# A delta-rule recurrence whose inverse times v is added up in PSUM, diagonal blocks placed by ScalarE, and a first channel product in 15 for 18 block products in three chunks

## The chip, the cores and the metric

The kernel runs on one core of one Trainium2 chip. The metric is device time of the whole program in microseconds, as the median of repeated runs; lower is better. Lines L... are lines of the kernel before, unless "of after" is said.

## The reference

The program is an attention block of delta-rule type and a mixer behind it, all in float32. B = 4 batches, H = 8 heads, S = 768 tokens, D = 48; the model width is H * D = 384, the hidden width 1536.

```python
k_n = k / (norm(k) + 1e-6)
state = 0                                   # per batch and head, D x D
for t in range(S):
    y[t] = q[t] @ state
    state += beta[t] * outer(k_n[t], v[t] - k_n[t] @ state)
x = y, heads side by side                   # (B, S, 384)
u = x + (x.T @ U @ V).T                     # U: S x 32, V: 32 x S
out = u + relu(u @ w_ch1) @ w_ch2           # 384 -> 1536 -> 384
```

## The kernel before

**The recurrence.** The tokens of a batch are cut into 12 chunks of 64 (c = 0 to 11); six chunks make a unit, and the units are n = 0 to 7, two per batch. A unit is loaded (`load`), its keys and queries are turned (`turn`, `turn_blocks`) and multiplied into 64 x 64 blocks (`products`, L700 to L746), the blocks' triangular systems are inverted (`blocks`, L814 and L820 on VectorE; `joins`, L871 to L932 on TensorE), and the inverses are put together in `pg` (`diagonals`, L950; L938). `products` also picks the 32 x 32 diagonal blocks out of PSUM into `diag`: ScalarE takes the even ones through a mask (L721), VectorE adds the odd ones through another mask (two instructions, L724), and after it ScalarE copies the whole product (L731), which gives the PSUM banks back.

`prepare` (L1024 to L1062) multiplies, for three chunks at a time, the inverses with the keys (L1034, copied by ScalarE at L1053) and with the values (L1045, copied by ScalarE at L1058 over `vn`). `recur` (L1064 to L1125) then goes through the chunks: 8 small matmuls of state with keys (L1083), VectorE subtracts them from the prepared values into `z` (L1096), 8 matmuls of z with keys (L1111), VectorE adds them to the state (L1122). `outputs` (L994 and L1008) multiplies the state and z with the queries beside it; `put` copies that into X on ScalarE (L978).

**The mixer.** `front` adds the low-rank part to X and turns a piece of 256 tokens (i = 0 to 2 of batch b; here called a chunk b.i) into `ut` (L1437 to L1483). For the chunks of batches 0 to 2, `wide` does the two channel products. The first (`channels`, L1537) is 12 blocks of 128 hidden channels by 3 blocks of the width by 256 tokens: 36 matmuls of 128x128 with 256 columns, two hidden blocks to a step; ScalarE applies the relu from PSUM into `hs` (L1502). `add_up` (L1560) makes sums S1 and S2 of `hs`, and `narrow` (L1645) does the second product in seven block products for eight (42 matmuls of 192 columns); `gather` (L1573) adds them to X. Batch 3 is done last, in another way: its first product is already made in 15 block products for 18 (`quick`, L1351), with sums of weights (`weight_sums`, L1292) and sums of tokens (`token_sums`, L1323), where each block product is read out of PSUM as soon as it is made, by ScalarE (L1376, L1365) or by VectorE, which adds it to another block (L1382); its second product is L1769.

**What sets the order.** Each piece of work is a Python generator that yields one step at a time: an engine, a PSUM bank to take, banks to give back. Which generator goes on next is written out by hand in one long list (`ORDER`, L144 on): at each position stands the name of a generator, and its next instructions are recorded there. So every engine's instruction order is fixed by that list; semaphores are put in where one engine reads what another wrote, and where two engines touch the same bank of PSUM. PSUM has 8 banks: up to four pairs for the recurrence and the products (three once the mixer runs), and two single ones ("mix", banks 6 and 7) for the mixer.

**Forms on TensorE.** The mixer's matmuls use the whole 128 x 128 array. The recurrence's use quarters of 64 x 64, four at a time, and `joins` sixteenths of 32 x 32. A float32 matmul appears in the trace as two records, each with its weight load (PEld).

Of the kernel before, what the change touches and what calls it, by code (L numbers as in the profile page):

```python
# [17 lines left out]
BK = 32  # L18
SB = 16
DP = 64  # L20
GT = 256
# [6 lines left out]
def kernel(  # L28
# [116 lines left out]
    add_up b0 i0 f00: 594 612 668; add_up b0 i0 f03: 632 645 667; add_up b0 i1 f00: 793 820 841; add_up b0 i1  # L145
    f03: 846 859 861; add_up b0 i2 f00: 1028 1035 1036; add_up b0 i2 f03: 1037 1045 1046; add_up b1 i0 f00: 1165
    1167 1194; add_up b1 i0 f03: 1200 1202 1206; add_up b1 i1 f00: 1324 1351 1354; add_up b1 i1 f03: 1359 1362
    1366; add_up b1 i2 f00: 1511 1513 1548; add_up b1 i2 f03: 1541 1543 1556; add_up b2 i0 f00: 1679 1693 1740;
    add_up b2 i0 f03: 1704 1719 1738; add_up b2 i1 f00: 1868 1869 1872; add_up b2 i1 f03: 1889 1893 1900; add_up
    b2 i2 f00: 2004 2039 2048; add_up b2 i2 f03: 2049 2051 2054; blocks n0: 61 73 75 76 82 84 86 88 89 91 93 94  # L150
    96 97 103 110 114 122; blocks n1: 143 157 160 163 173 175 179 192 201 206 208 212 213 215 218 219 226 229;
    blocks n2: 479 498 510 513 514 518 520 524 526 528 529 532 536 538 539 541 542 544; blocks n3: 691 708 710
    711 714 716 718 720 721 722 733 740 744 748 752 755 756 760 768 769 771 785 788 792 794 797 798 799 800 801
    802 824 825 826; blocks n4: 937 941 942 944 948 951 964 965 966 967 975 977 979 1003 1004 1009 1017 1019
    1038 1067 1084 1085 1086 1088 1114 1115 1116 1117 1118 1119 1120 1121 1122 1138; blocks n5: 1143 1171 1173
    1174 1175 1204 1217 1221 1231 1232 1243 1244 1245 1257 1262 1266 1274 1277 1286 1287 1289 1292 1293 1294
    1295 1300 1304 1307 1309 1325 1332 1348 1349 1350; blocks n6: 1484 1490 1491 1492 1505 1506 1516 1527 1532
    1536 1540 1549 1554 1573 1579 1583 1584 1588 1592 1607 1608 1612 1617 1632 1636 1643 1645 1646 1647 1649
    1650 1664 1671 1673; blocks n7: 1676 1695 1696 1703 1711 1712 1720 1737 1741 1747 1749 1773 1778 1779 1784
    1786 1788 1792 1797 1807 1810 1811 1813 1817 1818 1819 1822 1825 1826 1827 1828 1841 1842 1848; channels b0  # L160
    i0 e0: 546 547; channels b0 i0 e1: 551 552; channels b0 i0 e2: 553 555; channels b0 i0 e3: 556 567; channels
    b0 i0 e4: 568 588; channels b0 i0 e5: 597 600; channels b0 i1 e0: 738 743; channels b0 i1 e1: 759 761;
    channels b0 i1 e2: 775 778; channels b0 i1 e3: 796 805; channels b0 i1 e4: 822 829; channels b0 i1 e5: 830
    832; channels b0 i2 e0: 924 927; channels b0 i2 e1: 932 934; channels b0 i2 e2: 936 939; channels b0 i2 e3:
    960 972; channels b0 i2 e4: 992 994; channels b0 i2 e5: 995 1008; channels b1 i0 e0: 1131 1132; channels b1
    i0 e1: 1133 1134; channels b1 i0 e2: 1136 1144; channels b1 i0 e3: 1158 1160; channels b1 i0 e4: 1161 1166;
    channels b1 i0 e5: 1184 1185; channels b1 i1 e0: 1278 1282; channels b1 i1 e1: 1284 1310; channels b1 i1 e2:
    1311 1313; channels b1 i1 e3: 1314 1315; channels b1 i1 e4: 1323 1333; channels b1 i1 e5: 1343 1344;
    channels b1 i2 e0: 1455 1458; channels b1 i2 e1: 1477 1479; channels b1 i2 e2: 1489 1493; channels b1 i2 e3:
    1494 1495; channels b1 i2 e4: 1503 1504; channels b1 i2 e5: 1520 1524; channels b2 i0 e0: 1641 1642;  # L170
    channels b2 i0 e1: 1653 1654; channels b2 i0 e2: 1655 1667; channels b2 i0 e3: 1681 1682; channels b2 i0 e4:
    1683 1684; channels b2 i0 e5: 1686 1687; channels b2 i1 e0: 1814 1816; channels b2 i1 e1: 1835 1836;
    channels b2 i1 e2: 1837 1840; channels b2 i1 e3: 1844 1845; channels b2 i1 e4: 1846 1847; channels b2 i1 e5:
    1871 1874; channels b2 i2 e0: 1947 1948; channels b2 i2 e1: 1955 1974; channels b2 i2 e2: 1981 1990;
    channels b2 i2 e3: 2002 2011; channels b2 i2 e4: 2022 2029; channels b2 i2 e5: 2037 2041; cut f0 f00 k0 to1:
    2153; cut f0 f00 k1 to0: 2182; cut f0 f00 k1 to1: 2123; cut f0 f00 k2 to0: 2171; cut f0 f00 k2 to1: 2186;
    cut f1 f03 k0 to1: 2206; cut f1 f03 k1 to0: 2244; cut f1 f03 k1 to1: 2251; cut f1 f03 k2 to0: 2241; cut f1
    f03 k2 to1: 2245; cut f2 f06 k0 to1: 2169; cut f2 f06 k1 to0: 2181; cut f2 f06 k1 to1: 2130; cut f2 f06 k2
    to0: 2168; cut f2 f06 k2 to1: 2170; cut f3 f09 k0 to1: 2220; cut f3 f09 k1 to0: 2243; cut f3 f09 k1 to1:
    2242; cut f3 f09 k2 to0: 2247; cut f3 f09 k2 to1: 2249; diagonals n0 h0: 188 190 191 195 210 222; diagonals  # L180
    n0 h1: 167 169 171 176 181 186; diagonals n1 h0: 312 315 319 336 343 353; diagonals n1 h1: 290 292 303 338
    349 358; diagonals n2 h0: 598 599 622 628 634 638; diagonals n2 h1: 647 651 672 697 703 724; diagonals n3
    h0: 863 890 891 892 893 899; diagonals n3 h1: 879 880 881 889 931 933; diagonals n4 h0: 1151 1159 1176 1193
    1205 1208; diagonals n4 h1: 1180 1224 1225 1228 1239 1254; diagonals n5 h0: 1391 1392 1393 1410 1411 1412;
    diagonals n5 h1: 1364 1396 1416 1420 1443 1471; diagonals n6 h0: 1714 1715 1724 1742 1757 1768; diagonals n6
    h1: 1709 1710 1716 1744 1746 1756; diagonals n7 h0: 1919 1921 1922 1928 1929 1930; diagonals n7 h1: 1857
    1859 1860 1884 1906 1907; front b0 i0: 495 502 503 515 516 519; front b0 i1: 523 561 591 602; front b0 i2:
    636 652 678 682; front b1 i0: 1058 1059 1068 1070 1076 1078; front b1 i1: 1108 1153 1196 1210; front b1 i2:
    1381 1403 1424 1426; front b2 i0: 1587 1591 1610 1614 1624 1635; front b2 i1: 1639 1644 1668 1690; front b2
    i2: 1751 1761 1764 1775; front b3 i0: 2038 2040 2042 2045 2046 2052; front b3 i1: 2053 2057 2060 2062; front  # L190
    b3 i2: 2063 2068 2071 2073; gather b0 i0 h0 c0 k0: 677; gather b0 i0 h0 c0 k1: 680; gather b0 i0 h0 c1 k6:
    737 871; gather b0 i0 h1 c0 k2: 693; gather b0 i0 h1 c0 k5: 734 926; gather b0 i0 h1 c1 k3: 706; gather b0
    i0 h1 c1 k4: 715; gather b0 i1 h0 c0 k0: 862; gather b0 i1 h0 c0 k1: 847; gather b0 i1 h0 c1 k6: 916 925;
    gather b0 i1 h1 c0 k2: 873; gather b0 i1 h1 c0 k5: 913 1170; gather b0 i1 h1 c1 k3: 876; gather b0 i1 h1 c1
    k4: 887; gather b0 i2 h0 c0 k0: 1031; gather b0 i2 h0 c0 k1: 1066; gather b0 i2 h0 c1 k6: 1110 1281; gather
    b0 i2 h1 c0 k2: 1075; gather b0 i2 h1 c0 k5: 1111 1296; gather b0 i2 h1 c1 k3: 1082; gather b0 i2 h1 c1 k4:
    1087; gather b1 i0 h0 c0 k0: 1203; gather b1 i0 h0 c0 k1: 1229; gather b1 i0 h0 c1 k6: 1270 1623; gather b1
    i0 h1 c0 k2: 1233; gather b1 i0 h1 c0 k5: 1272 1560; gather b1 i0 h1 c1 k3: 1237; gather b1 i0 h1 c1 k4:
    1258; gather b1 i1 h0 c0 k0: 1365; gather b1 i1 h0 c0 k1: 1375; gather b1 i1 h0 c1 k6: 1448 1689; gather b1
    i1 h1 c0 k2: 1405; gather b1 i1 h1 c0 k5: 1449 1707; gather b1 i1 h1 c1 k3: 1409; gather b1 i1 h1 c1 k4:  # L200
    1423; gather b1 i2 h0 c0 k0: 1578; gather b1 i2 h0 c0 k1: 1572; gather b1 i2 h0 c1 k6: 1634 1798; gather b1
    i2 h1 c0 k2: 1593; gather b1 i2 h1 c0 k5: 1631 1688; gather b1 i2 h1 c1 k3: 1606; gather b1 i2 h1 c1 k4:
    1615; gather b2 i0 h0 c0 k0: 1731; gather b2 i0 h0 c0 k1: 1739; gather b2 i0 h0 c1 k6: 1808 1870; gather b2
    i0 h1 c0 k2: 1762; gather b2 i0 h1 c0 k5: 1812 2134; gather b2 i0 h1 c1 k3: 1776; gather b2 i0 h1 c1 k4:
    1781; gather b2 i1 h0 c0 k0: 1901; gather b2 i1 h0 c0 k1: 1892; gather b2 i1 h0 c1 k6: 1940 2072; gather b2
    i1 h1 c0 k2: 1913; gather b2 i1 h1 c0 k5: 1942 2216; gather b2 i1 h1 c1 k3: 1916; gather b2 i1 h1 c1 k4:
    1918; gather b2 i2 h0 c0 k0: 2050; gather b2 i2 h0 c0 k1: 2058; gather b2 i2 h0 c1 k6: 2088 2218; gather b2
    i2 h1 c0 k2: 2067; gather b2 i2 h1 c0 k5: 2086 2197; gather b2 i2 h1 c1 k3: 2070; gather b2 i2 h1 c1 k4:
# [1689 lines left out]
```

## Time and profile before

| | |
|---|---|
| median of 3 runs | 589.99 us (589.21 to 590.24) |
| the profiled execution | 589.53 us |
| its span in the trace | 587.7 us |
| instructions | 23435 |
| granted TensorE clock, mean of the span | 0.944 |

The span is the time from the first to the last instruction of the trace; 1.8 us of the execution lie outside it. A busy TensorE in the page is not TensorE at its peak: the ends of matmuls are modelled, and in the records a matmul's time reaches into the next one's. For its pace one takes the distance from start to start, or the length of a run of equal instructions in the chain of waits, divided by their count. In the page's table of 40 slices one slice is 14.7 us.

### The profile page before, as it was taken

How to read it: one execution, taken by the hardware profiler on the slowest of the kernel's cores; microseconds unless marked ns; L12 is line 12 of the kernel's file. 1: busy time of each engine (PE TensorE's matmuls, PEld its weight loads, DVE VectorE, ACT ScalarE, POOL GpSimd, SP SyncE). 2: the span in 40 equal slices, each digit the busy share in tenths (PEclk: the TensorE clock that was granted, in tenths of full speed). 3: DMA queues.
4: the chain of work that ended last, by engine and by line, in shares of the span. 5: the costliest groups of instructions: out<-in, count | busy, mean ns of one | idle time of the engine just before them, and what ended most of it. 6: DMA issues, size and time to landing. Idle time of an engine off the chain costs nothing.

```text
span 587.7 us, 23435 instructions
## 1 busy us (share of the span) xinstructions
PE 553.4 (94%) x10404; PEld 476.9 (81%) x10404; DVE 441.9 (75%) x1051; ACT 217.9 (37%) x444; POOL 133.4 (23%) x229
## 2 busy tenths in 40 slices
PE   3788887899999999999999999999999999999996
PEld 3688876588989987989989888899889868755996
DVE  3888757899998587897885479999874225789941
ACT  2846575526323432054134331144333421345000
POOL 8122045044016406042041405044030000000000
PEclk9665567999999999999999999999999999999999
DMA  9960638532015216022220404231020000100001
GB/s 142 196 164 24 217 91 203 123 86 45 14 25 105 53 35 113 11 53 55 53 47 13 81 16 90 56 89 34 3 66 30 3 3 1 41 0 2 0 15 67
DMA packets 89396, 36.21 MB, mean 62 GB/s; under 512 B 75408, under 2 KB 87056, under 8 KB 89296
## 3 DMA queue, kind: packets, MB, share of 16 engines
q1 hardware_dynamic: 80752, 24.69, 19.9%
q0 software_dynamic: 6944, 9.74, 7.6%
q8 instruction: 81, 1.33, 1.0%
q10 hardware_dynamic: 1600, 0.30, 0.3%
q14 instruction: 19, 0.16, 0.1%
HBM read 29.98 MB, written 4.72 MB: 59 GB/s over the span
## 4 chain that ended last, share of the span: by engine, by line
PE 81%; DVE 12%; issue 2%; ACT 2%; DMA 1%; SPq 0%; DVEq 0%; ACTq 0%
PE P L1537 23%; PE P L1645 21%; PE P L1769 7%; PE P L1351 6%; PE P L711 4%; PE P L1083 2%; DVE xt L820 2%; DVE prod L814 2%; PE P L1111 2%; PE P L885 2%; PE P L871 2%; PE P L1045 2%; PE P L1008 2%; PE P L1034 2%; PE P L994 2%
## 5 line engine op out<-in xcount | busy, mean ns | idle before, releaser
L1537 PE MATMUL P<-ut,w_sb 128*128 128x256 f32 x648 | 151.3, 386 | 0.0
L1537 PEld LDWEIGHTS P<-ut,w_sb 128*128 128x128 f32 x648 | 119.6, 190 | 17.9 <-issue 1.2
L1645 PE MATMUL P<-w_sb,hs 128*128 128x192 f32 x540 | 94.1, 329 | 0.0
L1645 PEld LDWEIGHTS P<-w_sb,hs 128*128 128x128 f32 x540 | 87.5, 190 | 2.6 <-issue 1.2
L820 DVE TENSOR_TENSOR xt<-xt,prod 128x112 f32<-128x112 f32 (+21 forms) x200 | 64.6, 323 | 6.9
L814 DVE TENSOR_TENSOR prod<-gs,xt 128x112 f32<-128x112 f32 (+21 forms) x200 | 63.4, 317 | 3.6
L1502 ACT ACTIVATE hs<-P 128x512 f32<-128x512 f32 x54 | 32.1, 596 | 80.4 <-PE P L1537 69.3
L978 ACT COPY X<-P 64x192 f32<-64x192 f32 x96 | 30.0, 313 | 72.4 <-PE P L1008 71.2
L566 POOL DMA_DIRECT2D slot<-in_v_dram x32 | 21.1, 666 | 75.9 <-DVE prod L814 49.7
L1645 PE MATMUL P<-w_sb,S 128*128 128x192 f32 x216 | 38.0, 330 | 0.0
L1096 DVE TENSOR_TENSOR z<-slot,P 128x192 f32<-128x192 f32 x44 | 15.5, 353 | 29.8 <-PE P L1083 29.2
L1645 PEld LDWEIGHTS P<-w_sb,S 128*128 128x128 f32 x216 | 34.8, 190 | 2.1 <-issue 1.2
L1573 DVE TENSOR_TENSOR X<-X,P 128x192 f32<-128x192 f32 x63 | 21.5, 346 | 18.6 <-PE P L1645 18.1
L552 POOL DMA_DIRECT2D slot<-in_k_dram x40 | 25.0, 630 | 44.3 <-DVE z L1096 22.4
L950 ACT COPY slot<-zz 32x384 f32<-32x384 f32 x64 | 32.3, 508 | 3.0 <-DVE zz L889 2.1
L711 PEld LDWEIGHTS P<-slot 48*64 48x64 f32 x1536 | 29.3, 151 | 4.7 <-issue 1.9
L711 PE MATMUL P<-slot 48*64 48x64 f32 x1536 | 32.4, 238 | 0.7 <-DVE slot L742 0.7
L566 POOL DMA_DIRECT2D slot<-in_k_dram x44 | 29.7, 677 | 7.9 <-PE P L1111 7.6
L957 POOL MEMSET slot<- 32x384 f32 x32 | 13.0, 411 | 72.3 <-PE P L914 70.2
L552 POOL DMA_DIRECT2D slot<-in_q_dram x40 | 24.5, 619 | 18.6 <-DVE slot L758 10.5
L799 POOL MEMSET xt<- 128x1056 f32 x8 | 7.9, 984 | 86.9 <-DVE zz L827 86.8
L1122 DVE TENSOR_TENSOR s<-s,P 128x192 f32<-128x192 f32 x40 | 13.9, 348 | 13.0 <-PE P L1111 10.1
(180 smaller groups left out, 1001.5 us busy)
## 6 DMA issues: line engine op xcount, KB each, us to landing
w_sb<-in_moe_w_ch_dram SPq DMA_DIRECT2D x10, 384.0 KB, 5.5
out_dram<-X SPq DMA_DIRECT2D x19, 192.0 KB, 2.5
slot<-in_k_dram SPq DMA_DIRECT2D x48, 72.0 KB, 3.4
slot<-in_k_dram POOLq DMA_DIRECT2D x44, 72.0 KB, 3.3
slot<-in_v_dram SPq DMA_DIRECT2D x32, 72.0 KB, 3.3
slot<-in_v_dram POOLq DMA_DIRECT2D x32, 72.0 KB, 2.8
X<-in_moe_w_ch_dram SPq DMA_DIRECT2D x6, 384.0 KB, 4.5
wide<-in_moe_w_ch_dram SPq DMA_DIRECT2D x6, 384.0 KB, 5.1
```

What stands on the lines that cost most here:

```text
L552: queue.dma_start(out=blocked(n)[quarter(y % 4), j, g, :, 0:w], in_=src[b, 4 * g + 2 * j + par, hf * UC * L : (hf + 1) * UC * L, BK * low ...
L566: queue.dma_start(out=t[half(1 - g if name == "z" else g), :, to, 0:D], in_=src[b, 4 * g + s, hf * UC * L : (hf + 1) * UC * L, :].rearrang ...
L711: nc.tensor.matmul(p_g[half(g ^ (par * i)), par, c], kq[rows, c, j, 0, half(g)], kq[rows, c, j, i, half(g)], start=True, stop=True,)
L814: nc.vector.tensor_tensor(out=prod, in0=gb[:, :, j : j + 1, j + 1 :].to_broadcast([128, split, m, w]), in1=xb[:, :, 0:m, j : j + 1].to_bro ...
L820: nc.vector.tensor_tensor(out=xb[:, :, 0:m, j + 1 :], in0=xb[:, :, 0:m, j + 1 :], in1=prod, op=ALU.subtract,)
L950: nc.scalar.copy(pg[quarter(i), :, at, :, a : a + BK], cut(zc, h)[quarter(i)].rearrange("p r (c j) t -> p r c j t", j=2),)
L978: nc.scalar.copy(x[half(c % 2), c // 2, 4 * D * g : 4 * D * (g + 1)].rearrange("p (j r d) -> p r j d", r=2, d=D), states(p_y)[half(g)],)
L1351: nc.tensor.matmul(to, forms[h][w][:, g] if isinstance(w, str) else w1_of(*w, h)[:, g], TOKENS[t] if isinstance(t, str) else u_of(*t), sta ...
L1502: nc.scalar.activation(hs[:, fs[0] : fs[1] + 1 : fs[1] - fs[0]], p_f, ACTF.Relu)
L1537: nc.tensor.matmul(p_f[:, x], w(x, t), ut[:, t], start=(t == 0), stop=(t == KT - 1))
L1645: nc.tensor.matmul(to, of[0], of[1], start=of[2], stop=of[3], skip_group_check=True)
L1769: nc.tensor.matmul(p[:, m], a[:, h, 128 * m : 128 * m + 128], v[:, h, j], start=fresh and m == h == j == 0, stop=(j == h == 1), skip_group ...
```

## The change

For batches 1 to 3 (`JOINT = 1`), and units n from 2, three things are done otherwise; in three chunks of the mixer a fourth.

1. `prepare` no longer multiplies the inverses with the values, and the copy of the keys' product gets a factor of -1. A new part `values(c)` makes that product chunk by chunk, straight into the PSUM bank in which `recur` then adds its own 8 matmuls. VectorE's subtraction into z is replaced by a ScalarE copy out of PSUM. The matmuls of z with keys go into other columns of the bank that the next chunk's `values` has taken, so no bank of their own is taken.
2. For units n from 3, the diagonal blocks are copied by four ScalarE instructions of 32 partitions, in place of one masked ScalarE instruction and two on VectorE.
3. Chunk 2.2's first channel product is made in 15 block products for 18 for both halves of the hidden blocks, chunks 1.2 and 2.1 for one half (`FAST`). Each block product is two matmuls of 128 columns (`fifteen`), into one bank per half, where two chains of sums take 256 columns each; each is read at once by ScalarE or VectorE (`seen`), relus are separate ScalarE instructions on `hs` (`limit`), and the sums of tokens are made by 8 VectorE instructions per chunk in S1 and S2 (`tokens`). The sums of weights are those that batch 3 uses.
4. `ORDER` is written anew from position 497 on: 2479 positions for 2326.

```diff
@@ products (units n > 2)
-                yield op("act", act(384) + 0.1, rush=True)
-                nc.scalar.mul(to, p_g[:, :, :, 0:BK], even[:, 0:1])
-                for r in range(2):
+                if n > NU * JOINT:
+                    for y in range(4):
+                        a = BK * (y % 2)
+                        yield op("act", act(384))
+                        nc.scalar.copy(to[quarter(y)], p_g[quarter(y), :, :, a : a + BK])
...
@@ prepare
+            if n >= NU * JOINT:
+                yield op("act", act(768), give=[("pair", x)])
+                nc.scalar.mul(
+                    kq[:, cs[0] : cs[2] + 1, :, 0].rearrange("p c j (g t) -> p (c j) g t", g=2),
+                    p_k.rearrange("p g c j t -> p (c j) g t"), -1.0,
+                )
+                emitted(("ready", n, h), 0.1)
+                return
@@ recur
+        def values(c):
...
+            x = yield op("pe", 0.23, "Q", take="pair", words=32, flow=0.16)
+            sums[c] = x
+            for j, par, g in heads:
+                nc.tensor.matmul(
+                    states(pair(x)[:, :, 0 : 2 * D])[half(g ^ par), par, j],
+                    zt[half(g), par, cu, j],
+                    vn[half(g), cu, 2 * par + j],
+                    start=(j == 0),
+                    stop=(c == 0),
+                    skip_group_check=True,
+                )
+            emitted(("values", b, c))
...
+            if b >= JOINT:
+                yield need(("values", b, c))
+                xb = sums[c]
+                p_b = pair(xb)[:, :, 0 : 2 * D]
+                if c > 0:
...
+                        nc.tensor.matmul(
+                            states(p_b)[half(g ^ par), par, j],
+                            kq[half(par, D), cu, j, 0, half(g)],
+                            states(s_old)[half(par, D), g, j],
+                            start=False,
...
+                yield op("act", act(192), give=[("pair", xb)], rush=True)
+                z = zs[c] = small.tile([128, 4, D], FP32, name="z", bufs=3)
+                nc.scalar.copy(z.rearrange("p (r j) d -> p r (j d)", r=2), p_b)
...
+                if b >= JOINT:
+                    yield need(("values", b, c + 1))
+                    p_s = pair(sums[c + 1])[:, :, 2 * D : 4 * D]
@@ the mixer's first product
+    FAST = {(1, 2): (0,), (2, 1): (0,), (2, 2): (0, 1)}
+    CHAINS = (
+        ((4, 0, 1, 1), (10, 2, 0, -1), (12, 1, 0, 1), (13, 1, 0, 1), (2, 1, 1, -1), (7, 0, 1, -1), (14, 2, 1, 1),
+         (5, 2, 0, -1), (11, 0, 0, 1)),
+        ((1, 1, 1, 1), (6, 0, 1, 1), (9, 1, 1, 1), (0, 1, 0, -1), (3, 2, 0, 1), (8, 2, 1, -1)),
+    )
+    OPENING, PUT = (4, 10, 13), (12, 14, 4, 1, 10)
...
+        def fifteen(h, k):
+            bank = h if len(quickly) == 2 else 0
...
+            p = mixed(bank)[:, GT * k : GT * k + GT].rearrange("p (g n) -> p g n", g=2)
+            for z, (e, r, m, sign) in enumerate(CHAINS[k]):
...
+                    *[("seen", b, i, h, CHAINS[k][z - 1][0])] * (z > 0),
...
+                yield op("pe", 0.432, "F", take=("mix", bank) if z == k == 0 else None, words=8)
+                for g in range(2):
+                    nc.tensor.matmul(
+                        p[:, g],
...
+                        start=e in OPENING and g == 0, stop=g == 1, skip_group_check=True,
+                    )
...
+        def seen(h, e, p, r, m, sign, give):
+            to = hs[:, HF * h + r : HF * h + r + 4 : 3, 128 * m : 128 * m + 128]
+            if e == 11:
...
+                nc.scalar.activation(to, p, ACTF.Relu)
...
+            elif e in PUT:
+                yield op("act", act(256), rush=True)
+                nc.scalar.mul(to, p, float(sign))
...
+                begin(limit(h, r, m, to), 3)
+            else:
+                yield need(("put", b, i, h, r, m))
+                yield op("dve", dve(256), rush=True)
+                nc.vector.tensor_tensor(out=to, in0=to, in1=p, op=ALU.add if sign > 0 else ALU.subtract)
...
+        def limit(h, k, j, at):
...
+            yield op("act", act(256))
+            nc.scalar.activation(at, at, ACTF.Relu)
```

Counted in the two built programs, in instructions: on TensorE 72 matmuls of 128x128 with 256 columns go and 120 with 128 columns come; the 288 matmuls of the inverses with the values are as many as before, in groups of 8 for 24. On VectorE 33 subtractions into z and 20 masked additions go, 36 reads of block products and 24 sums of tokens (8 per chunk) come. On ScalarE 12 copies of prepared values, 10 masked diagonal copies and 12 relus go; 36 copies into z, 40 diagonal copies, 20 copies, 20 relus and 4 relus out of PSUM of block products come. DMAs are the same in number and size. TensorE changes between forms (whole array, quarters, sixteenths) 162 times for 169; its order is the same up to the first matmul of the mixer's first product.

More of the change, by code (lines that the diff above doesn't have):

```diff
@@ L155 @@
[L155 to L159, printed above, removed]
@@ L1062, in prepare @@
             emitted(("ready", n, h), 0.1)
+        sums = {}
+        def values(c):
+            n, cu = NU * b + c // UC, c % UC
+            _, _, zt, _, _, vn, _, _ = units[n]
+            yield need(
+                *[x for h in [cu // 3] for x in (("upper", n, h), ("diagonal", n, h))],
+                ("grams", n), ("scaled", n), *[("placed", b, c - 2)] * (c > 1),
+            )
[11 more added lines that the diff above has]
+            emitted(("values", b, c))
         zs = {}
+        if b >= JOINT:
+            for c in range(NC):
+                begin(values(c), 60)
         for u in range(NU):
@@ new lines, in limit, with rows, add_up @@
+        def limit(h, k, j, at):
+            yield need(*[("seen", b, i, h, x) for c in CHAINS for x, r, m, _ in c if (r, m) == (k, j)])
+            yield op("act", act(256))
+            nc.scalar.activation(at, at, ACTF.Relu)
+            for g in range(2):
+                emitted(("h", b, i, HF * h + 3 * g + k, j), 0.06)
+        def rows(k, m, f0=0, n=HF):
+            return [("h", b, i, HF * k + f, m) for f in range(f0, f0 + n)]
+        def add_up(f0):
+            yield need(
+                *rows(0, 1, f0, 3), *rows(1, 1, f0, 3), *rows(0, 0, f0, 3),
+                *[("made", b, i, h, e) for h in quickly for e in (8, 11)],
+            )
@@ L1638, in narrow @@
             else:
-                for x, y in enumerate(ys):
-                    if x:
+                for z, (x, y) in enumerate(turns):
+                    if z:
                         yield need(*SECOND[y][2])
@@ L1652, in narrow @@
                 emitted(("narrow", b, i))
-        for e in range(len(PAIRS)):
+        begin(made())
+        for e in range(len(plain)):
             begin(channels(e), 95)
+        for h in quickly:
+            for k in range(2):
+                begin(fifteen(h, k), 95)
+        for f0 in range(0, HF, 3):
+            begin(add_up(f0), 4)
         begin(last_sum(), 4)
@@ L1857 @@
             for i in range(NG):
+                if (b, i) in FAST:
+                    begin(tokens(b, i), 97)
                 begin(wide(b, i), 95)
```

562 lines of the change are left out of this document (333 added, 229 removed).

## The prediction

> **What bounds the kernel now.** I read the page first, then the chain of waits in order of time, the groups by form, the waits of TensorE, and one step of the timeline.
>
> ```profile
> PE 553.4 (94%) x10404; PEld 476.9 (81%) x10404; DVE 441.9 (75%) x1051; ACT 217.9 (37%) x444; POOL 133.4 (23%) x229
> ...
> PE   3788887899999999999999999999999999999996
> ...
> DVE  3888757899998587897885479999874225789941
> ...
> PEclk9665567999999999999999999999999999999999
> ...
> PE 81%; DVE 12%; issue 2%; ACT 2%; DMA 1%; SPq 0%; DVEq 0%; ACTq 0%
> ```
>
> From the ninth slice on TensorE is never under 9 tenths, at full clock. That alone does not say that it works and does not wait. The pace of equal runs does; here is the chain of waits for the whole span:
>
> ```profile
> 360.20 1.41 PE P L711 x96
> ...
> 464.45 1.49 PE P L1537 x6
> ...
> 467.27 1.49 PE P L1537 x6
> ...
> 487.85 0.66 PE P L1480 x6
> ...
> 521.34 22.33 PE P L1351 x68
> 543.66 37.06 PE P L1769 x228
> 581.16 2.23 PE P L1769 x12
> ```
>
> A record of 192 columns takes 37.06 / 228 = 0.1625 us, one of 384 columns 22.33 / 68 = 0.328 with a gap or two, one of 128 columns (L1480, transposes) 0.66 / 6 = 0.11. The line through these is 0.833 ns a column and 2.5 ns, so 256 columns take 0.216 and 128 take 0.109. Six records of L1537 should then last 1.30, and each of the short runs lasts 1.49: a change of form costs 0.19 to 0.20.
>
> With these paces I add up TensorE from the first matmul of L1537, at 114.92, to the end of the last of L1769, at 583.39:
>
> ```profile
> 114.92 9.33 PE L1537 MATMUL P<-ut,w_sb 128*128 128x256 f32 x42
> ```
>
> 648 records of L1537 at 0.216 are 140.0; 756 of L1645 and 240 of L1769 at 0.1625 are 161.9; 120 of L1351 at 0.3225 are 38.7; 2176 matmuls in quarters, two records each at the 14.7 ns of L711 (1.41 / 96) and some longer, are 69; sixteenths, transposes and the 32-column form, at their own runs' paces, another 26; 145 changes of form at 0.2 are 29. The sum is 464.6, and the stretch is 468.5. So only some 4 us of it are waits. What the change does to the time is what it does to TensorE's own stream, and what waits it puts into it; work of the other engines counts only through such waits.
>
> **Part 1, the first product in 15 for 18.** 72 matmuls of 256 columns go: 144 records at 0.216 are 31.1 us. 120 of 128 columns come: 240 records. Whether they run at 0.109 the trace of before does not show, since each needs its own weight load:
>
> ```profile
> L1537 PE MATMUL P<-ut,w_sb 128*128 128x256 f32 x648 | 151.3, 386 | 0.0
> L1537 PEld LDWEIGHTS P<-ut,w_sb 128*128 128x128 f32 x648 | 119.6, 190 | 17.9 <-issue 1.2
> ...
> L711 PEld LDWEIGHTS P<-slot 48*64 48x64 f32 x1536 | 29.3, 151 | 4.7 <-issue 1.9 <-ACT slot L698 1.3 <-DVE slot L742 0.9
> ```
>
> A load record is 190 ns long, but its length is no pace: the loads of L711 are 151 ns long, and a quarter takes one each 59 ns (four quarters at 14.7), with 64 columns of weights and 64 of data, where the stream alone would ask for 53. So load and stream overlap when they are equally long, at a cost of about 6 ns. I take 0.112 for the record of 128 columns: 240 are 26.9. Bounds: 26.2 (0.109) and 45.6 (0.190). Part 1 is worth -4.2 us (-4.9 to +14.5). The Trainium skill, page "TensorE: Matmul & The Clock Gate", section "LDWEIGHTS (loading the stationary operand)", puts a load at columns over 1.2 per ns, 107 ns for 128; as an estimate from it load and stream are level, and the sum would be -4.9.
>
> **Part 2, changes of form.** In the built program they are 162 for 169, all seven after 114.92: -1.4 us (0 to -1.4).
>
> **Part 3, the recurrence.** The matmuls are the same in number, so TensorE's work is unchanged. What can change is the wait between them:
>
> ```profile
> PE P L1008 <- DVE z L1096: 1.2, 4, 0.3
> PE P L994 <- DVE s L1122: 1.1, 2, 0.6
> ...
> PE P L1083 <- DVE s L1122: 1.0, 3, 0.5
> ...
> PE P L1111 <- DVE z L1096: 0.8, 2, 0.5
> ```
>
> One step, in the timeline:
>
> ```profile
> 465.88 0.45 PE L1083 MATMUL P<-s,slot 48*64 48x48 f32 x16
> ...
> 466.46 0.35 DVE L1096 TENSOR_TENSOR z<-slot,P 128x192 f32<-128x192 f32 x1 [1.53 <-PE P L1083]
> ...
> 466.87 0.40 PE L1111 MATMUL P<-z,slot 64*48 64x48 f32 x16
> ```
>
> Here z starts 0.13 after the matmuls end (466.33), lasts 0.35, and 0.06 later TensorE goes on. Two groups of outputs (0.23 each) stand between and cover 0.46 of these 0.54. After, a ScalarE copy out of PSUM takes the subtraction's place, and `values` (0.23) is a third group that mostly stands there.
>
> ```profile
> L950 ACT COPY slot<-zz 32x384 f32<-32x384 f32 x64 | 32.3, 508 | 3.0 <-DVE zz L889 2.1
> ...
> L978 ACT COPY X<-P 64x192 f32<-64x192 f32 x96 | 30.0, 313 | 72.4 <-PE P L1008 71.2
> ...
> L1096 DVE TENSOR_TENSOR z<-slot,P 128x192 f32<-128x192 f32 x44 | 15.5, 353 | 29.8 <-PE P L1083 29.2
> ...
> L724 DVE SCALAR_TENSOR_TENSOR slot<-P,even,slot 128x192 f32<-128x192 f32 x32 | 12.0, 406 | 6.7 <-ACT slot L721 6.7
> ...
> L1058 ACT COPY slot<-P 128x576 f32<-128x576 f32 x16 | 10.2, 638 | 0.9 <-PE P L1045 0.7
> ...
> L721 ACT ACTIVATE slot<-P,even 128x384 f32<-128x384 f32 x16 | 9.2, 582 | 23.0 <-PE P L711 22.8
> ```
>
> The copy takes 0.313 for 0.353, so the way is 0.50 against 0.69 of cover: the wait for z goes. Of the 4.1 us in those four rows about half belong to batches 1 to 3: -2.0 us (0 to -3). ScalarE gets 36 x 0.313 = 11.3 more and 12 x 0.638 = 7.7 less; VectorE loses 33 x 0.353 = 11.6. What is late next is a ScalarE copy that stands behind something long; that is a rival below.
>
> **Part 4, the diagonal blocks.** 20 VectorE instructions at 0.406 go (8.1 us); ScalarE gets 40 at about 0.5 (row L950, from SBUF) and loses 10 at 0.582: +14. No TensorE instruction is added. In `products` the four copies (2.0) stand where 0.58 + 2 x 0.41 = 1.4 stood, so a pair of banks is held 0.6 longer, ten times. I cost it at nothing, since other work stands on TensorE meanwhile; without that cover 10 x 0.6 = 6 us (0 to +6).
>
> **Part 5, the waits that the 15 products bring.** This is the part against the change. Each product is read before the next of its chain overwrites it, and both chains of a half lie in one bank. In the built program a product waits for the reads of that bank that stand before it in the written order, the other chain's too. The Trainium skill, page "PSUM — Partial Sum Buffer", section "PSUM bank collisions raise a hardware error", says why: two engines must not touch one bank and quadrant at once, whatever the address. No run here shows a collision. What a read costs when nothing covers it:
>
> ```profile
> L1382 DVE TENSOR_TENSOR slot<-slot,P 128x384 f32<-128x384 f32 x36 | 19.0, 550 | 5.4 <-PE P L1351 2.9 <-ACT slot L1376 2.1
> ...
> L1376 ACT ACTIVATE slot<-P 128x384 f32<-128x384 f32 x20 | 9.1, 489 | 16.7 <-PE P L1351 16.7
> ```
>
> Between 0.35 for 192 columns and 0.55 for 384, a VectorE read of 256 is 0.42 (ScalarE 0.37). With 0.13 before and 0.06 after, an uncovered read stops TensorE for 0.6 us. In the order of after most of the 60 products have 1.3 us of L1537's successor or a group of the recurrence between; five wait for the read of the product right before them (one at the start and one later in chunk 1.2, one in 2.1, two in 2.2), and two have a single product (0.45) between. That is 5 x 0.6 + 2 x 0.15 = 3.3 us. Reads also queue: VectorE is full where chunk 1.2 is made, and in 2.2 the reads stand in front of the state's addition, for which the recurrence waits.
>
> ```profile
> 360.00:380.00 20.00, 20.00 (x326) 16.77 (x318) 19.20 (x48) 2.74 (x6) 1.45 (x3) 1.00 0.33 69
> 380.00:400.00 20.00, 19.88 (x227) 17.25 (x227) 18.56 (x51) 10.32 (x20) 8.41 (x14) 1.00 0.35 79
> 460.00:480.00 20.00, 19.70 (x539) 15.72 (x540) 7.20 (x20) 7.60 (x20) 0.00 (x0) 1.00 0.01 3
> ```
>
> (The columns after the length are TensorE, its loads, VectorE, ScalarE.) Chunk 1.2's 9 reads and 8 sums of tokens (128 to 384 columns, on the line through rows L1096 and L1382) are 3.8 + 3.1 = 6.9 us of VectorE where 1 or 2 in 20 are free, against 4.2 of subtractions gone per batch. Chunk 2.2 falls into the third row, where VectorE has 12 us of 20 free. I put 1.7 on this queueing: part 5 is +5.0 us. Bounds: +1 (most of the five covered by work that the profile can't show) and +12 (each of some twenty tight products stops TensorE once).
>
> **The sum.** -4.2 - 1.4 - 2.0 + 0 + 5.0 = -2.6. The profiled execution took 589.53, so 586.9; it lies 0.46 under the median of 589.99, so on the median's footing 587.4. The stretch before 114.92, where TensorE shows 3 to 8 tenths, is left as it is; TensorE's order is the same there.
>
> **The rivals.**
>
> (a) *The reads of the 15 products bound three chunks.* In one bank TensorE and readers take turns, so a product costs 0.45 + 0.6 unless other work stands between. The gain of parts 1 to 3 is 7.6 us, so it decides from 13 uncovered products on (13 x 0.6 = 7.8). At 20 of 60 it is +12 - 7.6 = +4.4: 594 us, slower. For it: the full VectorE of 360 to 400, and the waits across chains in the built order. Against it: the order puts L1537's successor or the recurrence between most pairs. Chance 0.19.
>
> (b) *Loads pace the short matmuls* at 0.190 a record: 240 x 0.078 = 18.7 more, 606 us. Against it L711's 59 ns. Chance 0.03.
>
> (c) *The waits do not come*: the reads are all covered, part 5 is +1 or less. 589.99 - 7.6 + 1 = 583.4. For it: the stretch of before has only 4 us of waits in 468, so an order written in this way can hide nearly all. Chance 0.15.
>
> (d) *ScalarE becomes late.* Before z now stand diagonal copies (four at 0.5), copies of 0.8, relus. If one z in five comes 0.5 late, 7 x 0.5 = 3.5, and the gain is down to about nothing: 590.5 (589 to 591). This is also how the recurrence's part would not do what it says. For it: ScalarE goes from 217.9 to about 245 us, strictly in order. Against it: 245 of 588 is not much. Chance 0.16.
>
> **How the numbers follow.** The forecast, 587.4 (585 to 588.8), has 0.47. A measurement of this kernel tells about 0.2%, 1.2 us, from no change: faster is below 588.8, slower above 591.2. Faster: forecast and (c), 0.62. Same: (d), 0.16. Slower: (a) and (b), 0.22. The range has to hold 8 in 10: it leaves out (b), the lower end of (c) and the upper half of (a): 583 to 592.
>
> **What would show it.** Part 1: the new line's matmuls start 0.109 to 0.115 apart; at 0.19, (b). Part 3: TensorE's waits for z on ScalarE are all but absent; if they sum to 3 us or more, (d). Part 5: TensorE's waits for `hs` (the reads) sum to about 5; at 12 or more (a), at 1 (c). TensorE's sum from the first matmul of the first product to the last of the kernel should be about 459 us of work. The prediction is wrong in its ground if the waits are as said and the time is not: then something in the stretch before, or VectorE's 12% in the chain, was moved by the new order.

## The result, and the profile after

The changed kernel is slower: 594.03 us median of 11 runs (592.80 to 598.09) beside 589.99 for the kernel before on the same chip (11 runs too, 589.21 to 593.74). The ratio is 1.007, with a 95% interval of 1.0051 to 1.0089, so +4 us where -2.6 was forecast. From here on line numbers are those of the kernel named beside them; the new product is L1711 in the changed kernel, and its reads are L1725 and L1730 on ScalarE and L1736 on VectorE. The profiled execution took 592.80 us, with a span of 590.9.

The page of the changed kernel, in the places that were shown of the one before (busy time by engine; TensorE and VectorE in 40 slices; the engines' shares of the chain that ended last):

```profile
PE 550.0 (93%) x10500; PEld 479.4 (81%) x10500; DVE 446.5 (76%) x1058; ACT 241.6 (41%) x530; POOL 132.9 (22%) x229
...
PE   4888887899999999999999999999989899999997
...
DVE  3888758999997369999873779998775435789933
...
PE 60%; DVE 5%; ACT 1%; issue 1%; SPq 1%; DMA 0%; DVEq 0%; ACTq 0%
```

TensorE is less busy over a longer span, and it now has two slices under 9 tenths late in the row, at 428 to 443 and 458 to 473 us, where the kernel before had none. Chunks 2.1 and 2.2 are made there. The granted clock is 1.00 in every stretch of 10 us from 120 to 580 in both kernels, so the clock is not it.

Both traces are cut at the same instructions: the first matmul of the mixer's first product; the first matmul of `front`'s 32-column form in batches 1, 2 and 3; the first matmul of the last batch's first product and of its second. "Work" is TensorE's instructions by the paces and changes of form of the prediction.

| stretch | before, elapsed | work | left over | after, elapsed | work | left over |
|---|---|---|---|---|---|---|
| to batch 1's `front` | 117.5 | 116.7 | 0.8 | 117.3 | 116.3 | 1.0 |
| to batch 2's (chunk 1.2 begins in it) | 129.1 | 129.1 | 0.0 | 126.2 | 122.9 | 3.3 |
| to batch 3's (2.1 and 2.2) | 119.7 | 118.7 | 1.0 | 129.2 | 120.1 | 9.1 |
| to the last first product | 22.1 | 22.5 | -0.4 | 21.7 | 22.1 | -0.4 |
| to the last second product | 40.1 | 38.7 | 1.4 | 38.8 | 38.7 | 0.1 |
| sum | 428.6 | 425.7 | 2.9 | 433.2 | 420.1 | 13.1 |

The work column is worked out and not measured, so its fall of 5.6 us is the forecast's own figure for parts 1 and 2; that the time follows it is shown by the kernel without reads further down. What is left over, waits, rose by 10.2, nearly all of it (11.4) where products in 15 are made. The waits of TensorE in the changed kernel from 115 to 509 us (line that waits, engine and line waited for, us in total, times, longest):

```profile
PE P L1711 <- DVE hs L1736: 3.5, 5, 0.9
PE P L1711 <- ACT hs L1730: 2.4, 4, 1.2
PE P L1027 <- ACT X L1011: 1.1, 1, 1.1
PE P L1027 <- ACT hs L1730: 0.9, 1, 0.9
PE P L1847 <- DVE X L1774: 0.4, 1, 0.4
PE P L1149 <- DVE s L1217: 0.3, 1, 0.3
PE P L1041 <- ACT z L1163: 0.2, 1, 0.2
...
```

Ten waits are for reads of the products, 6.8 us in all: nine of products, and one of a matmul of `outputs` (L1027), where the view names ScalarE's read as what ended last. The one wait for z is 0.2. The 1.1 for a copy into X has to do with neither: that copy had itself waited 1.20 us for the store of X to `out` (a DMA). The same view of the kernel before, in the same part of the span, has 1.1 us in all:

```profile
PE P L1008 <- DVE z L1096: 0.9, 3, 0.3
PE P L871 <- DVE zz L827: 0.2, 1, 0.2
```

Now one piece of the timeline of the changed kernel, in chunk 2.2. The bracket is the idle time before the instruction and what ended it:

```profile
458.01 0.71 PE L1711 MATMUL P<-S,w_sb 128*128 128x128 f32 x4
458.82 0.38 ACT L1730 ACTIVATE hs<-P 128x256 f32<-128x256 f32 x1 [1.11 <-PE P L1711]
...
459.26 1.16 PE L1711 MATMUL P<-S,w_sb 128*128 128x128 f32 x8 [0.53 <-ACT hs L1730]
...
460.45 0.38 ACT L1730 ACTIVATE hs<-P 128x256 f32<-128x256 f32 x1 [1.25 <-PE P L1711]
460.73 0.31 ACT L1163 COPY z<-P 128x192 f32<-128x192 f32 x1
460.93 0.32 ACT L1011 COPY X<-P 64x192 f32<-64x192 f32 x1
461.14 0.39 ACT L1730 ACTIVATE hs<-P 128x256 f32<-128x256 f32 x1
...
461.58 0.71 PE L1711 MATMUL P<-S,wide 128*128 128x128 f32 x4 [1.17 <-ACT hs L1730]
```

A product of four records starts at 458.01; its read begins 0.81 later, and the next product starts 0.06 after the read ends. So the two starts lie 1.25 apart, where 0.45 is work. At 461.58 it is worse: the read that TensorE waits for stands on ScalarE behind a copy of z and a copy into X.

### The profile page after: what moved, and what is told of

Read it like the earlier page. It is cut to its first block, busy times and chain, and to the rows that moved or that the text cites. A ratio compares the mean times of both kernels' runs of the same rounds, so it can differ in the third digit from the quotient of the medians.

```text
span 590.9 us, 23673 instructions
## 1 busy us (share of the span) xinstructions
PE 550.0 (93%) x10500; PEld 479.4 (81%) x10500; DVE 446.5 (76%) x1058; ACT 241.6 (41%) x530; POOL 132.9 (22%) x229
## 4 chain that ended last, share of the span: by engine, by line
PE 60%; DVE 5%; ACT 1%; issue 1%; SPq 1%; DMA 0%; DVEq 0%; ACTq 0%
PE P L1847 18%; PE P L1681 12%; PE P L1977 7%; PE P L1487 7%; PE P L1711 5%; PE P L1027 1%; PE P L736 1%; PE P L1117 1%; PE P L1149 1%; PE P L1067 1%; PE P L1041 1%; DVE hs L1736 1%; PE P L1616 1%; PE P L1592 1%; DVE prod L845 1%
## 5 line engine op out<-in xcount | busy, mean ns | idle before, releaser
L1681 PE MATMUL P<-ut,w_sb 128*128 128x256 f32 x504 | 117.2, 384 | 0.0
L1681 PEld LDWEIGHTS P<-ut,w_sb 128*128 128x128 f32 x504 | 92.9, 190 | 13.5 <-DVE xt L851 0.6
L1638 ACT ACTIVATE hs<-P 128x512 f32<-128x512 f32 x42 | 24.9, 596 | 35.1 <-PE P L1681 32.7
L988 POOL MEMSET slot<- 32x384 f32 x32 | 13.1, 414 | 99.0 <-PE P L945 97.1
L1217 DVE TENSOR_TENSOR s<-s,P 128x192 f32<-128x192 f32 x40 | 14.0, 350 | 22.6 <-PE P L1205 19.8
L591 POOL DMA_DIRECT2D slot<-in_k_dram x44 | 29.2, 667 | 7.9 <-PE P L1205 7.6
L1163 ACT COPY z<-P 128x192 f32<-128x192 f32 x36 | 11.4, 317 | 42.7 <-PE P L1149 32.1
L1736 DVE TENSOR_TENSOR hs<-hs,P 128x256 f32<-128x256 f32 x36 | 14.8, 417 | 17.6 <-PE P L1711 16.9
```

What stands on the lines that cost most here:

```text
L591: queue.dma_start(out=t[half(1 - g if name == "z" else g), :, to, 0:D], in_=src[b, 4 * g + s, hf * UC * L : (hf + 1) * UC * L, :].rearrang ...
L1638: nc.scalar.activation(hs[:, fs[0] : fs[1] + 1 : fs[1] - fs[0]], p_f, ACTF.Relu)
L1681: nc.tensor.matmul(p_f[:, x], w(x, t), ut[:, t], start=(t == 0), stop=(t == KT - 1))
```

## The experiments

Three theories were held against each other. A: TensorE and the readers of the products take turns in a bank, so a product that no other work of TensorE covers (fills the time of the turn) stops TensorE. B: ScalarE is late for the recurrence, with z and the diagonal copies. Q: the reads cost by their number, through the readers' queues, and not by where the products stand. Beside the medians I give the time from the first matmul of the mixer's first product to the first of the last second product ("the stretch": 428.6 before, 433.2 after), since what lies ahead of it varies by up to 5 us between profiled executions (it starts at 114.6 to 119.7). The kernel before has a median of 590.6 to 591.3 in these comparisons.

**Leaving out the reads.** Both kernels keep the order and all matmuls. In the first the 36 VectorE reads are left out, in the second all 60, so the hidden values are not the reference's. VectorE and ScalarE lose the reads' work with them.

```diff
-                nc.vector.tensor_tensor(out=to, in0=to, in1=p, op=ALU.add if sign > 0 else ALU.subtract)
@@ the second one also
-                nc.scalar.activation(to, p, ACTF.Relu)
-                nc.scalar.mul(to, p, float(sign))
```

> The changed kernel, same order, with the 36 VectorE reads of block products left out (hs then lacks those sums; products and ScalarE reads stay). Theory A: the waits of TensorE for these reads go, 3.5 us by the table of waits and as much again behind them: 587 to 590. Theory B: under 1 us, 593 to 594.

> The changed kernel, same order, with all 60 reads of block products left out, ScalarE's 24 too (hs keeps what stood there, relus on hs stay). Theory A: all that the 15 products cost beyond their work goes, 582.5 to 586. Theory B: ScalarE loses 24 x 0.38 = 9 us of work, so z comes a little sooner, 591 to 593.

Measured: 587.94 us (ratio to before 0.9945, 0.9918 to 0.9972) and 585.41 (0.9895, 0.9856 to 0.9933); the stretch is 427.3 and 423.0. So A holds, and B has nothing left to explain: without the reads the changed kernel has no more waits than the kernel before (423.0 elapsed, 420.1 of work, 2.9 left over, as before). The largest of them from 117 to 502 us, second kernel:

```profile
PE P L1027 <- ACT X L1011: 0.8, 1, 0.8
PE P L916 <- issue: 0.5, 1, 0.5
PE P L1041 <- ACT z L1163: 0.3, 1, 0.3
...
```

The reads cost 433.2 - 423.0 = 10.2 us, and everything else in the change gives 423.0 - 428.6 = -5.6. These runs do not yet part A from Q.

**z copied by VectorE.** If ScalarE were late with z, VectorE would relieve it.

```diff
-                nc.scalar.copy(z.rearrange("p (r j) d -> p r (j d)", r=2), p_b)
+                nc.vector.tensor_copy(out=z.rearrange("p (r j) d -> p r (j d)", r=2), in_=p_b)
```

> The changed kernel, same order, with the copy into z on VectorE in place of ScalarE (36 instructions of 0.35). Theory A: 593 to 596, since the reads' waits stay and VectorE is fuller. Theory B: z is no longer behind copies and relus on ScalarE: 588 to 591.

Measured: 602.61 (1.0208, 1.0166 to 1.0250), stretch 440.8. B's figure is missed by 12 us, and A's was too low by 7. The waits that were not there before are for z on VectorE:

```profile
PE P L1711 <- DVE hs L1736: 4.9, 7, 0.9
PE P L1041 <- DVE z L1163: 2.7, 3, 1.8
PE P L1711 <- ACT hs L1730: 2.0, 3, 1.0
PE P L1027 <- DVE z L1163: 1.2, 2, 0.9
...
```

VectorE's queue, busy for 76% of the changed kernel's span, is the wrong place, in this order, for something that the recurrence waits for; the change's choice of ScalarE for z was right.

**The diagonal blocks as before**, in the changed kernel's order.

```diff
-                        nc.scalar.copy(to[quarter(y)], p_g[quarter(y), :, :, a : a + BK])
+                        if y == 0:
+                            nc.scalar.mul(to, p_g[:, :, :, 0:BK], even[:, 0:1])
+                        elif y < 3:
+                            nc.vector.scalar_tensor_tensor(
...
```

> The changed kernel with the diagonal blocks placed as before (one ScalarE instruction and two VectorE instructions in place of four ScalarE copies), in the changed kernel's order. If part 4 was worth nothing, as predicted: 593 to 595. If the four ScalarE copies hold up something: 589 to 592. If they relieve VectorE, which the reads of the products need: 596 to 599.

Measured: 601.79 (1.0158, 1.0115 to 1.0202), stretch 438.6: above even the third guess. The waits for the reads are the same as in the changed kernel (3.5, 2.4 and 0.9); new are waits of the two products of the mixer for relus that ScalarE does late:

```profile
PE P L1686 <- ACT hs L1643: 1.8, 2, 1.3
PE P L1852 <- ACT hs L1643: 1.4, 1, 1.4
PE P L1852 <- DVE X L1779: 1.2, 3, 0.5
```

So the four copies do no harm here. That they gain 5 to 8 us cannot be read from this: the order was written for them, and the kernel before, with the old form in an order of its own, waits no more than the kernel without reads. In the three places the relu stands on ScalarE behind an instruction that waits for VectorE: once the copy of the whole product (L767), which waits 7.28 us for VectorE's masked addition, and twice an instruction on the norms (L655), which waits 2.00 and 5.00 us.

**No product in 15 at all**: 18 products again in all three chunks, their 72 matmuls spread evenly over the places of the 60 products; and the same **for chunk 2.2 alone**.

```diff
-    FAST = {(1, 2): (0,), (2, 1): (0,), (2, 2): (0, 1)}
+    FAST = {}
@@ or, for chunk 2.2 alone
+    FAST = {(1, 2): (0,), (2, 1): (0,)}
```

> The changed kernel without its 15 products: all nine chunks make the first product with 36 matmuls of 256 columns, put evenly where the products in 15 stood; recurrence and diagonal blocks stay as changed. Theory A (TensorE and the readers of the 15 products take turns in one bank, some 11 us of waits in three chunks): 594.0 - 11 of waits + 4.2 of work that comes back = about 587 (586 to 589), at or under the time before. Theory B (ScalarE, which now copies z and the diagonal blocks, is late for the recurrence): the waits stay, the work comes back: 594 to 598.

> The changed kernel with chunk 2.2 made from 18 products again (36 matmuls of 256 columns, spread evenly over the places of its 30 products; 30 products in chunks 1.2 and 2.1 stay). TensorE's work grows by half of part 1, 2.1 us. Theory A with the turns mostly in chunk 2.2, where two chains in each of two banks run between the steps of the recurrence (about 6 of the 11 us): 594.0 + 2.1 - 6 = 590 (589 to 592). Rival Q (the full VectorE of 360 to 400 us, that is chunk 1.2 and 2.1): the cost stays, 595 to 597.

Measured: 591.97 (1.0031, 1.0009 to 1.0053), stretch 429.6; and 591.50 (1.0011, 0.9984 to 1.0038), stretch 431.0. The first lies between the theories: TensorE's work in the stretch is 423.5 there, so some 6 us are waits, most of them (4.7) between the `front`s of batches 2 and 3, none for a read, several for ScalarE's z and X. An order that was not written for these steps has waits of its own, and this run decides little. The second came as A said: its work is 1.7 us more and the stretch 2.2 less, so chunk 2.2 held some 3.9 of the 10.2 us, less than the 6 that I had thought.

**One product behind the other.** This parts A from Q: the instructions and reads of the changed kernel, but the 15 products of chunk 2.1 in a row (positions in the written order).

```diff
-fifteen b2 i1 h0 k0: 1829 1839 1843 1857 1873 1896 1909 1934 1951
+fifteen b2 i1 h0 k0: 1910 1914 1916 1918 1922 1928 1932 1934 1938
-fifteen b2 i1 h0 k1: 1838 1858 1876 1890 1908 1938
+fifteen b2 i1 h0 k1: 1912 1920 1924 1926 1930 1936
```

> The changed kernel with only the written order altered: the 15 products of chunk 2.1 stand one directly behind the other, late in that chunk, each read before the next is written; the same instructions, the same reads, the other work moves up. Theory A (TensorE and the readers take turns in a bank, each product that no other work covers stops TensorE for about 0.6 us = 0.13 + 0.42 + 0.06): 14 uncovered products are 8.4 us, less the 2 or so that this chunk has already, so 6 to 7 more than the changed kernel's 594.0: 599 to 602. Rival Q (the number of reads counts, through the queues of VectorE and ScalarE, and not where the products stand): the reads are the same in number, 593 to 595.

Measured: 613.46 (1.0338, 1.0277 to 1.0399), stretch 449.4. Q is refuted: the number of reads is the same, and 16 us more are lost. But A's 6 to 7 is far too small, too. The timeline of this kernel (the product is L1703, VectorE's read L1728):

```profile
438.27 0.71 PE L1703 MATMUL P<-S,w_sb 128*128 128x128 f32 x4 [0.58 <-DVE hs L1728]
439.02 0.42 DVE L1728 TENSOR_TENSOR hs<-hs,P 128x256 f32<-128x256 f32 x1 [0.80 <-PE P L1703]
439.50 0.71 PE L1703 MATMUL P<-S,w_sb 128*128 128x128 f32 x4 [0.51 <-DVE hs L1728]
...
447.53 1.22 PE L1703 MATMUL P<-S,w_sb 128*128 128x128 f32 x4 [0.47 <-ACT hs L1722]
449.33 1.22 PE L1703 MATMUL P<-S,w_sb 128*128 128x128 f32 x4 [0.58 <-DVE hs L1728]
```

Two things are seen. First the true price: products start 1.23 apart (438.27 to 439.50). Four records stream for 0.45, the read begins 0.30 after that, lasts 0.42, and 0.06 later TensorE goes on: 0.78 us, and not 0.6. (Of the 0.30, 0.10 lies in the product itself: after a pause its second record starts 0.21 after the first, and not 0.11.) The view of waits lists 0.51 of it, since a matmul's record (0.71) reaches beyond its stream. Second, after 444.40 a product's record lasts 1.22, and the starts lie 1.7 to 1.8 apart. The same kernel by stretches of 5 us (TensorE, its loads, VectorE, ScalarE and POOL with counts; then the granted clock, the share of DMA and GB/s):

```profile
435.00:440.00 5.00, 2.95 (x19) 2.19 (x18) 0.84 (x2) 0.77 (x2) 0.00 (x0) 1.00 0.00 0
440.00:445.00 5.00, 2.94 (x18) 2.18 (x17) 1.69 (x4) 0.00 (x0) 0.00 (x0) 0.98 0.00 0
445.00:450.00 5.00, 3.43 (x13) 2.55 (x13) 0.84 (x2) 0.38 (x1) 0.00 (x0) 0.50 0.00 0
450.00:455.00 5.00, 4.49 (x14) 3.63 (x14) 2.83 (x7) 1.51 (x5) 0.67 (x1) 0.50 0.22 59
455.00:460.00 5.00, 4.97 (x31) 4.51 (x30) 0.65 (x2) 3.61 (x9) 0.00 (x0) 1.00 0.37 72
...
480.00:485.00 5.00, 3.83 (x106) 3.50 (x104) 0.09 (x1) 2.17 (x8) 0.00 (x0) 0.73 0.00 0
```

After 12 us in which TensorE streamed 0.45 of each 1.23 us, its granted clock fell to a half for some 10 us, and once more, for 3.4, in chunk 2.2. The Trainium skill, page "TensorE: Matmul & The Clock Gate", section "A second HAM failure mode: psum-queue depth-cycling", tells of a kernel in which short idles of TensorE between groups of matmuls make the clock gate swing between half and full; this trace agrees, with 0.50, though it shows two falls and no steady swing. The changed kernel itself never comes to that.

The 16 us are then made up like this, as an estimate: 14 turns at 0.78 are 10.9, of which the changed kernel already loses 2.9 in this chunk; the slow clock adds 3.6 (2.2 in the last five products, and 1.4 in the 12 records of L1673 behind them, which take 4.04 for 2.6); other waits that the view lists from 420 to 470 us are 2.4. Some 2 us were not followed.

**The second chain in the other bank.** The last kernel once more, but in chunk 2.1 the second chain of sums has a bank of its own.

```diff
+            alone = (b, i) == (2, 1)
-            bank = h if len(quickly) == 2 else 0
+            bank = h if len(quickly) == 2 else k * alone
...
-                        start=e in OPENING and g == 0, stop=g == 1, skip_group_check=True,
+                        start=e in (OPENING + (1, 6) * alone) and g == 0, stop=g == 1, skip_group_check=True,
```

> The kernel with the 15 products of chunk 2.1 one directly behind the other, with its second chain of products added up in the other bank (it starts its sums there itself); order, instructions and reads unchanged. 10 of the 14 neighbours are then of different chains and banks. Theory A: such a product has no read of the one before to wait for, only one of its own chain with a product (0.45) between: 4 x 0.78 + 10 x 0.33 = 6.4 where 10.9 was, and the granted clock falls less: 613.5 - 5 to 8: 605 to 609. If the readers' own pace or the chain of each sum sets it, not the bank: 611 to 615.

Measured: 600.89 (1.0169, 1.0144 to 1.0194), stretch 437.5, 11.9 less than with one bank. The row of 15 products, from 428.75 to the next product of the mixer (L1673):

```profile
428.75 1.57 PE L1704 MATMUL P<-S,w_sb 128*128 128x128 f32 x10
430.80 0.71 PE L1704 MATMUL P<-S,wide 128*128 128x128 f32 x4 [0.47 <-ACT hs L1723]
431.98 0.71 PE L1704 MATMUL P<-S,power 128*128 128x128 f32 x4 [0.47 <-ACT hs L1723]
432.53 1.46 PE L1704 MATMUL P<-S,w_sb 128*128 128x128 f32 x8
...
437.88 1.16 PE L1704 MATMUL P<-S,w_sb 128*128 128x128 f32 x8 [0.47 <-ACT hs L1723]
439.17 0.71 PE L1704 MATMUL P<-S,power 128*128 128x128 f32 x4
439.71 1.46 PE L1673 MATMUL P<-ut,w_sb 128*128 128x256 f32 x6
```

The row takes 11.0 us here and 19.8 with one bank (432.24 to 452.08). Only a product that follows one of its own chain still waits its full turn, four times; a change of chain costs some 0.1 ((11.0 - 15 x 0.45 - 4 x 0.78) / 10), and the clock stays at 1.00. So most of what two products waited for was the bank and not the data. The Trainium skill, page "PSUM — Partial Sum Buffer", section "PSUM bank collisions raise a hardware error", asks that engines be kept apart by bank and quadrant and not by address, and the built program does so. In the row that costs 8.8 us less the 2.2 of the slow clock, 6.6; the 11.9 of the whole stretch hold the rest of the slow clock too. No run here lets TensorE write into a bank while it is read, so these runs price the program's waits and not what would happen without them.

**The products moved apart.** Back to the changed kernel with one bank per half. Only the written order is altered: 57 of 2479 steps stand elsewhere, 26 of them products and 17 their reads and relus, so that other work of TensorE stands between a read and the next product of its bank. For one chain, for instance:

```diff
-fifteen b1 i2 h0 k0: 1515 1526 1540 1558 1582 1591 1601 1612 1638
+fifteen b1 i2 h0 k0: 1515 1533 1540 1558 1589 1600 1614 1629 1638
```

The second kernel is the same with all 60 reads left out, so its hidden values are not the reference's.

> The changed kernel, the same instructions and reads, with the written order altered: products, and a few steps about them, stand some places earlier or later, so that other work of TensorE stands between a read and the next product of its bank. Uncovered products were 1.22 us apart in the last run where 0.45 is their work, so one costs 0.78 us, not 0.6. Counted through the built order with the durations of the trace, some two thirds of the cost of the reads are covered now. Theory A: about 7 of the 10 us that the reads cost go: 587 (586 to 589), under the kernel before. Rival Q (the reads cost through the queues of the engines that read): 592 to 595.

> The last one with all 60 reads of the products left out (the outputs are not the reference's). In the changed kernel's order leaving them out was worth 8.6 us. Theory A: in the new order they are mostly covered, so it is worth 2 to 3: 584 to 586. If the reads cost by their number, it is worth 8 or more: under 580 if the order helped for another reason, or 585 beside an unhelped 594.

Measured: 587.31 (0.9946, 0.9925 to 0.9968), stretch 426.6; without reads 585.67 (0.9912, 0.9888 to 0.9936), stretch 426.1. Both as A said. The same change, in another order, is faster than both kernels, by 3.3 us than the one before; the reads, worth 10.2 us in the changed kernel, are worth 0.5 of the stretch (by the medians 1.6, where it was 8.6). The largest waits of TensorE from 115 to 505 us in the kernel with its reads:

```profile
PE P L1019 <- ACT X L1003: 1.1, 1, 1.1
PE P L1839 <- ACT hs L1717: 0.7, 1, 0.7
PE P L1673 <- ACT hs L1630: 0.3, 1, 0.3
...
```

No product (L1703) is in that view any more; the 0.7 is the one wait for a read that is left (L1717), of the mixer's second product. The rows left out are 0.3 and less. Q is refuted a second time.

Without its reads, the altered order takes 426.1 where the changed kernel's takes 423.0. Moving the steps gave back 3 us, and the trace tells where: the steps in their new places bring 14 more changes of form in the stretch (153 for 139, 11 of them beside a product that now stands among quarter matmuls), at 0.2 us each 2.8 as an estimate. So the cover is not free where the work put between has another form.

## Why the prediction was wrong, point by point

- **The ground held.** From the first mixer product on TensorE is the bound, and the time is its own work plus the waits put into it: -5.6 of work and +10.2 of waits make +4.6 in the stretch, beside +4.0 in the medians.
- **Part 1 was right** (-4.2). Four products in a row in the changed kernel start 0.55, 0.44 and 0.45 apart, four records each, so 0.11 a record behind the change of form; rival (b), 0.19, is refuted:

```profile
478.86 0.71 PE L1711 MATMUL P<-S,w_sb 128*128 128x128 f32 x4
479.41 0.61 PE L1711 MATMUL P<-ut,wide 128*128 128x128 f32 x4
479.85 0.61 PE L1711 MATMUL P<-S,gs 128*128 128x128 f32 x4
480.30 0.61 PE L1711 MATMUL P<-ut,gs 128*128 128x128 f32 x4
```

- **Part 2 was right as far as the sum tells** (-1.4): the trace has the seven changes of form less, parts 1 to 4 together gave -5.6, and parts 1 and 2 were -5.6.
- **Part 3 was mis-sized**: at most -0.7 for -2.0. The waits for z do go, and ScalarE is not late with it (0.2 us; rival (d) is out). But I put half of 4.1 us into batches 1 to 3, and two of those four rows, 2.1 us, are waits for the state, which the change does not shorten; of before's 1.1 us of waits in that part of the span 0.9 are for z. I had divided a table of the whole span instead of asking it for that part.
- **Part 4 held as far as the sum tells** (0): in the changed kernel's order no wait of TensorE is listed for a diagonal copy. No run prices these copies by themselves.
- **Part 5 is the step that failed**: the reads cost 10.2 us and not 5.0. The mechanism was the one named, taking turns in a bank, as rival (a) had it; price and count were both too small.
  - Price: 0.78, not 0.6, since I took the 0.13 between matmul and reader from quarter matmuls, measured from the end of a record; from the end of the stream of a whole-array product it is 0.30.
  - Count: by hand I found five uncovered products and two half covered, 3.3 us, and put 1.7 on queueing. Measured from start to start, beyond 0.11 a record and 0.2 for a change of form (the late second record after a pause counted in), the trace has twelve places that lose 9.6 us: four plain turns (3.2), two partly covered (0.9), five whose read began only after other work of VectorE or ScalarE (4.7), and the `outputs` matmul (0.8). The read before 433.97, for instance, began 1.9 us after its product's stream, behind a transpose of 2.07 on VectorE; the 461.58 above is another. So the late reads, which I had put down as 1.7 us of queueing, are the larger part of the error.
  - Rival (a) decides at 13 x 0.6 = 7.8. I gave it 0.19 because the order puts other work "between most pairs", which is true of most and says nothing of the twelve. That its 594 is the measured time is in part luck: it was 20 products at 0.6, 12 us, against a gain of 7.6, and the runs have 10.2 against 5.6.
- **The marker was read too kindly**: waits for reads of 6.8 us in the table lie between my 5 (forecast) and 12 (rival a), but an uncovered turn of 0.78 shows there as 0.51, so the 6.8 of ten waits stand for 9 to 10.

## What to carry to other kernels

Where an accumulator is read between two matmuls into its bank, count a full turn for each pair that stands close: stream end to reader, the read, and back (0.78 us here for 256 columns), and look in the readers' queues for what stands ahead of the read. The saving in matmul work is paid out only if something else of TensorE stands in each turn; here moving 57 of 2479 steps turned +0.7% into -0.5%, although it cost some 2.8 us of changes of form. Ask a table of waits for the part of the span that the change touches, and measure turns from start to start, not by the listed idle time.

## What the runs showed of the hardware that was not expected

- TensorE's granted clock fell to 0.50 for some 10 us, although no idle time listed before a product was over 0.6 us; it was enough that TensorE streamed 0.45 us in each 1.23 for 12 us. It stayed at 1.00 in the row with two banks (15 x 0.45 us in 11.0) and in the changed kernel, whose turns are scattered.
- A read of one bank does not hold up a product into the other: with two banks the row of 15 products took 11.0 us for 19.8, of which 2.2 are the slower clock.
- A product's record in the trace lasts 0.71 us at full clock where its stream takes 0.45, and its reader starts 0.04 after the record's end. After a pause the second record of a product starts 0.21 after the first, the others 0.11 apart.
